# Eight quarter transfers for the input weights, another order of the hand-written schedule for pairs 0 to 17, and value transfers without unread bytes

## The chip, the cores and the metric

The kernel runs on one core of a Trainium2 chip. The time is device time in microseconds (us), the median of three runs: 406.16 us (405.56 to 406.44). The profile is one execution seen by the hardware profiler.

## The reference

The attention is a cosine attention over 8 batches, 12 heads, 448 positions and 64 channels; it is followed by a feed-forward layer with a hard-swish.

```python
q_n = q / (np.linalg.norm(q, axis=-1, keepdims=True) + 1e-06)
k_n = k / (np.linalg.norm(k, axis=-1, keepdims=True) + 1e-06)
scores = np.matmul(q_n, k_n.transpose(0, 1, 3, 2)) / tau          # tau = 0.1
attn = np.exp(scores - max) ; attn = attn / (sum + 1e-09)
x = heads side by side of np.matmul(attn, v)                       # 3584 x 768
h = x @ w_in                                                       # 768 x 2048
return (h * np.clip(h + 3.0, 0.0, 6.0) / 6.0) @ w_out              # 2048 x 768
```

## The kernel before

**Units of work.** Two heads are handled together: a "pair". There are 6 pairs to a batch and 48 in all. The queries and keys come in as items: item j holds the queries or the keys of two neighbouring pairs (2 x 7 x 64 float32 values on each of 128 partitions), so pairs 0 and 1 need items 0 and 1, pairs 2 and 3 items 2 and 3, and so on.

**The steps of an item.** `load_qk` (LQ) fetches it, `square` (SQ) squares it on the engine that its letter names (a = ScalarE, p = GpSimd, v = VectorE) and over the chunks that its numbers name, `reduce` (RE) sums the squares on VectorE, `norms` (NO) turns the sums of two items into inverse norms with four small ScalarE activations, `normalise` (NM) multiplies, and `transposes` (TR) turns the item over on TensorE into a bank of PSUM. `copy_q`, `copy_k` and `copy_k3` (CQ, CK, CS) bring the result to SBUF. Items from 14 on are turned by a DMA instead (XD).

**The steps of a pair.** `scores` (SC, groups 0 to 3) multiplies keys by queries, `exps` (EX) takes the exponential on ScalarE, `values` (VA) multiplies by the values, which `load_v` (LV) fetched and `vcast` (VC) turned into bf16, `finish_values` (FI) divides by the sums on VectorE, and `back` with `copy_x` (BK, CX), or a DMA (XP, XB), puts the result into `xT`, the input of the feed-forward layer.

**The feed-forward layer.** A unit (U) of the stream is a `mm1_unit`, six matmuls for 128 of the 2048 hidden columns of one batch; UA is its ScalarE part and UV its VectorE part. The first can start only when all six pairs of batch 0 are in `xT`. Units 31 to 36 are `mm2_unit`s, which read `w_out`. W (`next_weights`) issues the next weight transfer, cast to bf16 on the way, from GpSimd's queue. A check while the program is built, in `mm1_unit`, says how many transfers must have been issued before a unit.

**Order.** Every engine runs its own instructions in the order in which they are issued. The order of pairs 0 to 17 is written out in the list `PLAN`, one word for each step with its numbers behind dots; from pair 18 on a loop issues the rest. DP and D (`busy_pv`, `busy`) are matmuls of zeros that nobody reads, 248 and 512 columns wide. OPEN ends the start: until then two score buffers (SC0 and SC1, two PSUM banks each) take the scores in turn, so that a score must wait for the exponential before the last; from then on the four banks and the banks Y and Z form a ring of six. The word SC.i.g.n names the score buffer n, TR.j.Y the bank Y.

**Memory.** All raw items, their squares and the raw values lie in one SBUF tile, `big`: seven places for items, two for squares (items of even and odd number), three for values. So SQ of item j must wait for RE of item j - 2, LQ of item j for NM of item j - 7, and LV of d (for pairs 2d and 2d + 1) for the casts of the values three before.

Of the kernel before, what the change touches and what calls it, by code (L numbers as in the profile page):

```python
# [8 lines left out]
FP32 = mybir.dt.float32  # L9
BF16 = mybir.dt.bfloat16  # L10
AF = mybir.ActivationFunctionType
# [50 lines left out]
def kernel(  # L62
# [76 lines left out]
    def raw_buffer(j):  # L139
# [4 lines left out]
    n2s = [const.tile([128, 2, 14], FP32, name=f"n2{i}", tag=f"n2{i}") for i in range(2)]  # L144
    rs = [
        [const.tile([128, 2, 14], FP32, name=f"{x}{i}", tag=f"{x}{i}") for x in ("ln", "nr", "le", "r")]
        for i in range(2)
# [19 lines left out]
    def needs(*what):  # L167
        for w in what:
            assert w in issued or any(x < 0 for x in w[1:] if isinstance(x, int)), w
# [31 lines left out]
    def load_v(d):  # L201
        needs(("VC", 2 * (d - NV)), ("VC", 2 * (d - NV) + 1))
        b, n = 2 * d // HP, 2 * d % HP
        for g in range(2):
            f = v[b, HP * g + n : HP * g + n + 2].rearrange("i (p c) d -> p i (c d)", c=7)
            t = vr[d % NV][:, 2 * g : 2 * g + 2, :, :].rearrange("p i c d -> p i (c d)")
            for half in range(2):
                o = t[64 * half : 64 * half + 64, :, (1 - half) * D : (5 - half) * D]
                nc.sync.dma_start(out=o, in_=f[:, :, 3 * half * D : (3 * half + 4) * D])
# [18 lines left out]
    def reduce(j, *heads):  # L228
# [6 lines left out]
        else:  # L235
# [3 lines left out]
            out=n2s[d % 2][:, j % 2, c],  # L239
# [6 lines left out]
    def norms(d, *items):  # L246
# [7 lines left out]
        ln, nr, le, r = (t[:, it, :] for t in rs[d % 2])  # L254
        nc.scalar.activation(out=ln, in_=n2s[d % 2][:, it, :], func=AF.Ln)
# [7 lines left out]
        for x in items:  # L263
            issued.add(("NO", d, x))

    def normalise(j, e, *heads):
# [10 lines left out]
            in1=rs[d % 2][3][:, j % 2, :]  # L277
# [36 lines left out]
    def transposes(j, bank=None):  # L314
        nrm = nrm_of.pop(j)
# [245 lines left out]
    def mm1_unit(b, fc):  # L561
        needs(*(("CX", i) for i in range(b * HP, (b + 1) * HP)))
        assert len(weights) <= 6 - 2 * (2 * fc // FCN)
# [534 lines left out]
```

## Time and profile before

| what | value |
|---|---|
| median of three runs | 406.16 us (405.56 to 406.44) |
| span of the profiled execution, first to last instruction | 403.1 us |
| median less that span | 3.06 us |
| TensorE matmul busy (PE) | 395.5 us, 98% |
| VectorE (DVE) / ScalarE (ACT) / GpSimd (POOL) busy | 286.4 / 278.3 / 234.0 us |
| mean granted TensorE clock | 1.000 |
| first transposes / first unit on PE | 10.17 / 42.85 us |

The profile gives no device time of its own for the profiled execution beyond its span; the 3.06 us are what lies around it in the timed runs, as far as can be told. Busy PE time counts the zero matmuls too (86 of DP, 10 of D). SP issues the plain DMAs and the DMA transposes; GpSimd issues the weights.

### The profile page before, as it was taken

The page shows a single profiled execution, that of the slowest core. Times are in us where ns is not written, and L with a number is a line of the kernel's source. Part 1 is how long each engine was busy: PE and PEld are TensorE (multiplying, and loading weights), DVE is VectorE, ACT ScalarE, POOL GpSimd, SP SyncE. Part 2 cuts the span into 40 slices and gives each one's busy share as a digit, 9 for nine tenths or more (in the row PEclk, how much of TensorE's full clock was granted, in tenths as well). Part 3 has the DMA queues.
Part 4 walks back from the last instruction along what each step waited for, and adds up shares of the span by engine and source line. Part 5 has one row for each costly group of instructions (what it writes and reads, how often), then busy time and mean ns, then how long its engine had stood idle before and what let it go on. Part 6 is the DMA issues. An engine that isn't in the chain of part 4 may idle for free.

```text
span 403.1 us, 9619 instructions
## 1 busy us (share of the span) xinstructions
PE 395.5 (98%) x3696; PEld 234.3 (58%) x3696; DVE 286.4 (71%) x503; ACT 278.3 (69%) x609; POOL 234.0 (58%) x228
## 2 busy tenths in 40 slices
PE   7999999999999999999999999999999999999996
PEld 4666656555655556556555556555565556555563
DVE  5898768766998777776867888687656566644663
ACT  5999998798467686786858768668658755225230
POOL 7799655662384997488386865766665500510070
PEclk9999999999999999999999999999999999999999
DMA  8999989979988659786989659976963523130134
GB/s 289 281 254 257 216 247 230 156 125 230 187 213 220 139 128 228 171 222 130 180 216 212 152 130 164 182 192 145 192 154 76 112 46 67 41 79 21 26 73 99
DMA packets 91566, 65.32 MB, mean 162 GB/s; under 512 B 56064, under 2 KB 89984, under 8 KB 91520
## 3 DMA queue, kind: packets, MB, share of 16 engines
q1 hardware_dynamic: 87408, 58.02, 62.8%
q0 software_dynamic: 3712, 6.29, 9.0%
q8 instruction: 29, 0.48, 0.5%
q10 hardware_dynamic: 400, 0.39, 0.3%
q14 instruction: 17, 0.14, 0.1%
HBM read 47.19 MB, written 11.01 MB: 144 GB/s over the span
## 4 chain that ended last, share of the span: by engine, by line
PE 94%; DVE 3%; DMA 1%; ACT 0%; issue 0%; DVEq 0%; ACTq 0%
PE M L567 24%; PE M L740 17%; PE PV L462 13%; PE Y L567 6%; PE M L422 6%; PE Z L567 5%; PE Y L740 4%; PE Z L740 4%; PE M L614 3%; PE M L820 2%; PE Z L422 2%; PE PV L922 2%; PE Z L820 1%; PE Y L422 1%; DVE n L238 1%; PE SC L422 1%
## 5 line engine op out<-in xcount | busy, mean ns | idle before, releaser
L440 ACT ACTIVATE at<-M 128x448 bf16<-128x448 f32 x200 | 99.9, 568 | 16.4 <-PE M L422 14.4
L567 PE MATMUL M<-xT,w_in_sb 128*128 128x448 bf16 x522 | 110.8, 352 | 0.0
L567 PEld LDWEIGHTS <-w_in_sb 128*128 128x128 bf16 x768 | 72.0, 98 | 62.6 <-issue 2.8
L274 POOL TENSOR_TENSOR nrm<-big,r 128x896 bf16<-128x896 f32 (+1 forms) x48 | 79.5, 1662 | 26.1 <-ACT r L262 19.3
L576 ACT ACTIVATE u<-M,bias 128x448 bf16<-128x448 f32 x87 | 57.0, 655 | 25.2 <-PE M L567 24.8
L582 DVE SCALAR_TENSOR_TENSOR gT<-u,M 128x448 bf16<-128x448 bf16 x76 | 46.7, 618 | 36.8 <-ACT u L576 36.3
L226 POOL TENSOR_TENSOR big<-big 128x896 f32<-128x896 f32 (+3 forms) x39 | 63.9, 1641 | 10.9 <-DMA big<-in_k_dram 5.7
L462 PEld LDWEIGHTS <-at 128*128 128x128 bf16 (+1 forms) x1536 | 54.9, 97 | 22.8 <-issue 13.5
L462 PE MATMUL PV<-vx,at 128*128 128x65 bf16 (+1 forms) x1536 | 64.3, 194 | 0.2 <-DVE on L483 0.2
L238 DVE TENSOR_REDUCE n<-big 128x14 f32<-128x896 f32 (+1 forms) x50 | 51.7, 1041 | 5.6 <-ACT big L224 4.6
L379 POOL COPY km<-tT 64x128 bf16<-64x128 bf16 x34 | 12.8, 376 | 58.1 <-DMA tT<-nrm 45.1
L769 POOL TENSOR_TENSOR big<-big 128x384 f32<-128x384 f32 x11 | 11.8, 1076 | 54.6 <-ACT big L788 54.5
L740 PEld LDWEIGHTS <-gT 128*128 128x128 bf16 x288 | 27.8, 98 | 20.0 <-DVE gT L718 0.6
L740 PE MATMUL M<-w_out_sb,gT 128*128 128x384 bf16 x208 | 37.9, 326 | 0.1
L440 ACT ACTIVATE at<-Z 128x448 bf16<-128x448 f32 x49 | 27.7, 565 | 9.9 <-PE M L422 7.3
L483 DVE TENSOR_TENSOR on<-PV,rc 128x512 bf16<-128x512 f32 x48 | 33.2, 691 | 1.7
L293 POOL CAST vx<-big 128x512 bf16<-128x512 f32 x44 | 33.2, 757 | 1.2 <-DMA big<-in_v_dram 1.1
L422 PE MATMUL M<-tT,kz 64*128 64x448 bf16 (+1 forms) x175 | 31.6, 351 | 0.0
L740 PEld LDWEIGHTS <-gs 128*128 128x128 bf16 x224 | 21.5, 98 | 14.8 <-DVE gs L718 0.4
L567 PE MATMUL Y<-xT,w_in_sb 128*128 128x448 bf16 x132 | 28.6, 352 | 0.0
L440 ACT ACTIVATE at<-Y 128x448 bf16<-128x448 f32 x45 | 25.7, 570 | 3.1 <-PE Z L422 1.7
L740 PE MATMUL M<-w_sum,gs 128*128 128x384 bf16 x144 | 26.3, 326 | 0.0
(130 smaller groups left out, 561.7 us busy)
## 6 DMA issues: line engine op xcount, KB each, us to landing
big<-in_v_dram SPq DMA_DIRECT2D x96, 128.0 KB, 4.4
big<-in_k_dram SPq DMA_DIRECT2D x24, 448.0 KB, 4.9
big<-in_q_dram SPq DMA_DIRECT2D x24, 448.0 KB, 4.4
out_dram<-o SPq DMA_DIRECT2D x107, 96.0 KB, 2.2
w_in_sb<-in_moe_w_in_dram POOLq DMA_DIRECT2D x4, 768.0 KB, 10.2
w_out_sb<-in_moe_w_out_dram POOLq DMA_DIRECT2D x4, 768.0 KB, 9.2
tT<-nrm SPq DMA_TRANSPOSE x34, 3.3
xT<-on SPq DMA_TRANSPOSE x25, 3.8
```

Of the source, the lines that this page charges most:

```text
L226: engines[e].tensor_tensor(out=o, in0=i, in1=i, op=ALU.mult)
L238: nc.vector.tensor_reduce(out=n2s[d % 2][:, j % 2, c], in_=sq[:, :, :, :].rearrange("p g c d -> p (g c) d")[:, c, :], axis=AX.X, op=ALU.add,)
L274: engines[e].tensor_tensor(out=nrm[:, :, g, :].rearrange("p c g d -> p g c d"), in0=raw_of[j][:, g, :, :], in1=rs[d % 2][3][:, j % 2, :] . ...
L293: (engines[e].copy if e == "a" else engines[e].tensor_copy)(out=o, in_=f)
L422: nc.tensor.matmul(o, ks, qt[rows], start=True, stop=True)
L440: nc.scalar.activation(out=o, in_=x, func=AF.Exp, scale=inv_tau)
L462: nc.tensor.matmul(pv_out(j, h), at[rows, n, q_cols(i // HP, j)], vt[rows, 3 + h if name == "M" else 5 * h + int(name[1]), :], start=(name ...
L483: nc.vector.tensor_tensor(out=on[:, :, :, :].rearrange("p j h d -> p h j d"), in0=pv4[:, :, :, 0:D], in1=rc[:, :, :].to_broadcast([128, 2, ...
L567: nc.tensor.matmul(ps[:, 0:S], w_in_sb[:, cc, fc * 128 : (fc + 1) * 128], x[:, cc, 0:S], start=(cc == 0), stop=(cc == CC - 1),)
L576: nc.scalar.activation(out=u[:, :], in_=ps[:, 0:S], func=AF.Relu, bias=half_bias, scale=1.0 / 6.0)
L582: nc.vector.scalar_tensor_tensor(out=g[:, fc, c0 : c0 + S], in0=u[:, :], scalar=1.0, in1=ps[:, 0:S], op0=ALU.min, op1=ALU.mult,)
L740: nc.tensor.matmul(m, lhs[:, c, :], rhs[:, c, c0 : c0 + width], start=(base is None and c == 0), stop=(c == KC - 1), skip_group_check=True,)
```

## The change

- **Order.** `PLAN` is replaced. It has the same steps for pairs 0 to 17, with these differences: DP stands for 91 matmuls instead of 86 and D for 1 instead of 10; some squares are cut in two and given to two engines; SQ of items 6 and half of 7 and the second half of NM of items 1 and 5 are on VectorE; four norms (items 4 to 11) do their last two operations on VectorE (`NO.d.v`); the norms of items 12 to 15 and of 16 to 19 are taken four items at a time (the new `norms_two`, NN, on ScalarE and VectorE); seven CK and three CX are on ScalarE.
- **Weights.** `w_in` comes in eight transfers of a quarter of its columns (for each 64-row half) instead of four of a half, so W occurs twelve times. The check in `mm1_unit` follows.
- **Values.** `load_v` leaves out the 64 channels x 2 heads that `vcast` never reads: of the four transfers of each LV two bring 3 chunks instead of 4.
- **Norm tiles.** The small tiles of the norms for even and odd d lie in one tile each, padded from 14 to 16 columns.

```diff
@@ -19,42 +19,44 @@
 PLAN = [
-    "LQ.1 DP.5 SQ.1.a.11.3 SQ.1.p.4.3 DP.1 SQ.1.a.0.4 LQ.0 SQ.0.p.8.6 DP.2 DP.4 LQ.3 LQ.2 SQ.1.v.7.4 RE.1.1",
-    "SQ.0.a.0.6 RE.1.0 NO.0.1 LQ.5 LQ.4 SQ.0.v.6.2 DP.6 NM.1.p.0 D.10 RE.0.1 DP.3 NM.1.p.1 RE.0.0 DP.8 NO.0.0",
-    "SQ.3.a.0.7 LV.0 DP.2 SQ.2.a.0.7 NM.0.p.0 RE.3 RE.2 NM.0.p.1 TR.1.Y DP.2 TR.0.Z CK.0.v DP.4 SQ.4.p.0.7 CQ.0.v",
-    "SQ.5.a.0.7 LQ.6 NO.1 LV.1 LQ.7 SC.0.0.0 SC.0.1.1 DP.5 DP.3 CQ.1.v EX.0.0 RE.5 RE.4 NM.3.p SC.0.2.0 CK.1.v DP.3",
-    "EX.0.1 DP.3 EX.0.2 NM.2.v DP.3 SC.0.3.1 TR.3.Y LQ.8 NO.2 EX.0.3 DP.3 SC.1.0.0 TR.2.Z EX.1.0 VC.0.v SC.1.1.1 DP.2",
-    "EX.1.1 VA.0.0 CK.2.v VC.1.v VC.3.v NM.4.p NM.5.p VA.0.1 LQ.9 SC.1.2.0 SQ.6.a.0.7 LQ.11 DP.5 DP.2 SC.1.3.1 EX.1.2",
-    "CQ.2.v LQ.10 LV.2 VA.0.2 VA.0.3 DP.3 SC.2.0.0 DP.2 EX.1.3 CK.3.v SC.2.1.1 EX.2.0 TR.4.Y SC.2.2.0 SQ.7.p.0.7",
-    "EX.2.1 RE.6 FI.0 RE.7 LV.3 VA.1.0 SQ.8.p.0.7 SC.2.3.1 CQ.3.v VC.2.v CQ.5.v VA.1.1 EX.2.2 SC.3.0.0 EX.2.3 VA.1.2",
-    "NO.3 RE.8 SC.3.1.1 CQ.4.v EX.3.0 DP.2 DP.4 EX.3.1 VA.1.3 TR.5.Z SC.3.2.0 W SQ.9.p.0.7 EX.3.2 FI.1 CK.4.v BK.0.Y",
-    "VA.2.0 SC.3.3.1 RE.9 LV.4 EX.3.3 NO.4 VA.2.1 VA.2.2 VA.2.3 SC.4.0.0 EX.4.0 NM.6.p DP.2 SC.4.1.1 SQ.10.p.0.7 W",
-    "SQ.11.p.0.7 EX.4.1 CX.0.v TR.6.Y CK.5.v FI.2 CQ.7.v VA.3.0 BK.2.Z RE.10 SC.4.2.0 EX.4.2 NM.7.p CQ.6.v VA.3.1",
-    "SC.4.3.1 DP.2 EX.4.3 CX.2.v SC.5.0.0 RE.11 VA.3.2 EX.5.0 SC.5.1.1 VA.3.3 VC.4.p SC.5.2.0 FI.3 VC.5.p EX.5.1",
-    "BK.1.Y TR.7.Z SC.5.3.1 CX.1.v CK.6.v CK.7.v VA.4.0 EX.5.2 DP.2 CS.7.v EX.5.3 BK.3.Y VA.4.1 LQ.12 CS.6.v OPEN",
-    "DP.2 CX.3.v NO.5 SC.6.0 VA.4.2 VA.4.3 SC.6.1 SC.6.2 EX.6.0 NM.8.p FI.4 EX.6.1 EX.6.2 SC.6.3 TR.8 BK.4 VA.5.0",
-    "CX.4.v VA.5.1 CQ.8.v SC.7.0 VA.5.2 EX.6.3 NM.9.p CQ.9.v VC.6.p VA.5.3 SC.7.1 FI.5 EX.7.0 SC.7.2 TR.9 SC.7.3",
-    "NM.10.p CK.8.v VA.6.0 EX.7.1 EX.7.2 VC.8.p CS.8.v W BK.5 SQ.12.p.0.7 LQ.13 VA.6.1 VA.6.2 SC.8.0 EX.7.3 CS.9.v",
-    "VA.6.3 CK.9.v DP.1 EX.8.0 CX.5.v SC.8.1 SC.8.2 VC.7.p FI.6 LQ.15 EX.8.1 U UA SQ.13.a.0.7 LV.5 U TR.10 EX.8.2 UA",
...
+    "DP.2 DP.1 DP.1 DP.1 DP.3 DP.1 LQ.1 SQ.1.a.4.3 DP.2 DP.2 DP.2 DP.1 DP.1 SQ.1.p.11.3 DP.1 SQ.1.v.0.4 SQ.1.a.7.4",
+    "DP.2 LQ.0 DP.1 SQ.0.a.0.6 D.1 DP.3 LQ.3 DP.1 DP.1 DP.3 DP.2 DP.3 RE.1.0 DP.3 SQ.0.p.6.2 SQ.0.p.8.6 DP.1 RE.1.1",
+    "SQ.3.p.4.3 RE.0.0 LQ.2 DP.1 RE.0.1 NO.0.1 NM.1.p.0 NM.1.v.1 DP.1 DP.1 LQ.5 SQ.3.a.0.4 TR.1.Y NO.0.0 DP.1 DP.2",
+    "NM.0.p.1 DP.1 LQ.4 RE.3 DP.1 DP.1 DP.2 NM.0.p.0 SQ.2.a.0.7 RE.2 DP.1 DP.3 DP.1 TR.0.Z SQ.5.a.0.4 DP.2 DP.1",
+    "SQ.5.a.4.3 RE.5 CQ.0.v DP.1 DP.3 NO.1 DP.1 CK.0.a SQ.4.p.4.3 SC.0.0.0 SQ.4.a.0.4 EX.0.0 DP.4 LV.0 LQ.6 LQ.8",
+    "CK.1.v VC.0.v CQ.1.v SC.0.1.1 VC.1.v SC.0.2.0 EX.0.1 NM.3.p NM.2.p RE.4 SQ.6.v.0.7 DP.1 DP.1 DP.1 LQ.7 DP.1 DP.2",
+    "EX.0.2 SC.0.3.1 EX.0.3 SQ.7.p.4.3 NO.2.v NM.4.p TR.3.Y RE.6 SC.1.0.0 EX.1.0 SC.1.1.1 LV.1 VA.0.0 TR.2.Z SC.1.2.0",
+    "EX.1.1 CK.2.v CQ.2.v VA.0.1 NM.5.p.0 DP.1 EX.1.2 DP.1 W CQ.3.v LQ.9 VA.0.2 VA.0.3 FI.0 LQ.10 SQ.8.a.0.7 SC.1.3.1",
+    "CK.3.v EX.1.3 SC.2.0.0 VC.3.p DP.1 EX.2.0 SQ.7.v.0.4 RE.7 NM.5.v.1 DP.1 VA.1.0 W RE.8 SC.2.1.1 EX.2.1 DP.1",
+    "VA.1.1 DP.1 SC.2.2.0 SQ.9.p.0.7 DP.1 DP.2 SC.2.3.1 EX.2.2 EX.2.3 VA.1.2 DP.2 VC.2.v SC.3.0.0 NO.3.v SC.3.1.1",
+    "VA.1.3 DP.2 DP.1 SQ.10.p.0.7 DP.1 NM.6.p LV.2 VC.5.p FI.1 EX.3.0 EX.3.1 TR.5.Z RE.9 TR.4.Y CK.4.a SC.3.2.0 LQ.11",
+    "CQ.4.v EX.3.2 LQ.13 SQ.11.p.0.7 NM.7.p CQ.5.v SC.3.3.1 CK.5.v DP.1 NO.4.v VA.2.0 DP.1 VA.2.1 VA.2.2 LV.3",
+    "SC.4.0.0 VA.2.3 FI.2 EX.3.3 SC.4.1.1 TR.6.Y EX.4.0 BK.0.Z SC.4.2.0 RE.10 CQ.6.v DP.1 CX.0.v VC.4.p VA.3.0 EX.4.1",
+    "SC.4.3.1 VA.3.1 EX.4.2 EX.4.3 NM.8.p SC.5.0.0 SC.5.1.1 EX.5.0 VA.3.2 CQ.7.v VA.3.3 VC.7.p RE.11 FI.3 W BK.2.Y",
+    "TR.7.Z W SC.5.2.0 EX.5.1 SC.5.3.1 CK.6.v VA.4.0 CX.2.a CK.7.v BK.1.Y CS.7.v DP.1 CS.6.v EX.5.2 EX.5.3 LQ.12",
+    "BK.3.Z VA.4.1 CX.3.v NM.9.p OPEN LV.4 SC.6.0 VA.4.2 CX.1.v LQ.15 VA.4.3 FI.4 NO.5.v W SC.6.1 EX.6.0 LV.5 NM.10.p",
+    "SQ.13.p.0.7 SC.6.2 SC.6.3 TR.8 CQ.8.v EX.6.1 BK.4 CX.4.v EX.6.2 EX.6.3 VA.5.0 VA.5.1 LQ.16 VA.5.2 SQ.12.p.0.7",
+    "VC.6.v CQ.9.v SC.7.0 EX.7.0 VA.5.3 VC.9.p SC.7.1 SC.7.2 FI.5 LQ.14 TR.9 SC.7.3 CK.9.v NM.11.p CS.8.v CK.8.v",
+    "EX.7.1 VC.8.p VA.6.0 BK.5 VA.6.1 CS.9.v VA.6.2 CX.5.v VA.6.3 FI.6 EX.7.2 SC.8.0 U EX.7.3 TR.10 CQ.10.v EX.8.0",
+    "LV.6 VC.10.p UA UV SC.8.1 EX.8.1 CQ.11.v SC.8.2 EX.8.2 VA.7.0 VA.7.1 VA.7.2 W SC.8.3 VA.7.3 SC.9.0 U SC.9.1 FI.7",
+    "RE.12 LQ.18 EX.8.3 EX.9.0 XP.6 UA UV SC.9.2 U VA.8.0 EX.9.1 UA VA.8.1 TR.11 CK.10.a RE.13 EX.9.2 U UA CS.10.v",
+    "SC.9.3 CK.11.v UV UV SQ.15.p.0.7 CS.11.v EX.9.3 VA.8.2 VA.8.3 SQ.14.p.4.3 FI.8 U U UA UV UA VA.9.0 SC.10.0",
+    "SQ.14.a.0.4 VC.11.p LV.8 W W VC.12.p EX.10.0 U VA.9.1 UV RE.14 SQ.16.p.6.1 SC.10.1 UA SQ.16.p.0.6 UV EX.10.1",
+    "SC.10.2 RE.15 NN.6.v EX.10.2 NM.12.p RE.16 VA.9.2 LQ.17 VA.9.3 NM.13.p U UA U NM.14.p U SC.10.3 EX.10.3 UV U U",
...
 ]
@@ -141,10 +143,8 @@
 
     sqs = [item(NR + i) for i in range(2)]
     nrms = [const.tile([128, 7, 2, D], BF16, name=f"nrm{i}", tag=f"nrm{i}") for i in range(3)]
-    n2s = [const.tile([128, 2, 14], FP32, name=f"n2{i}", tag=f"n2{i}") for i in range(2)]
-    rs = [
-        [const.tile([128, 2, 14], FP32, name=f"{x}{i}", tag=f"{x}{i}") for x in ("ln", "nr", "le", "r")]
-        for i in range(2)
+    n2_and_r = [
+        const.tile([128, 2, 2, 16], FP32, name=x, tag=x)[:, :, :, 0:14] for x in ("n2", "ln", "nr", "le", "r")
     ]
     bias = const.tile([128, 2], FP32, name="bias", tag="bias")
     eps_bias, half_bias = bias[:, 0:1], bias[:, 1:2]
@@ -205,8 +205,11 @@
             f = v[b, HP * g + n : HP * g + n + 2].rearrange("i (p c) d -> p i (c d)", c=7)
             t = vr[d % NV][:, 2 * g : 2 * g + 2, :, :].rearrange("p i c d -> p i (c d)")
             for half in range(2):
-                o = t[64 * half : 64 * half + 64, :, (1 - half) * D : (5 - half) * D]
-                nc.sync.dma_start(out=o, in_=f[:, :, 3 * half * D : (3 * half + 4) * D])
+                n_c = 4 if g == half else 3
+                c0 = (7 - n_c) * half
+                x = 1 if g != half or half == 0 else 0
+                o = t[64 * half : 64 * half + 64, :, x * D : (x + n_c) * D]
+                nc.sync.dma_start(out=o, in_=f[:, :, c0 * D : (c0 + n_c) * D])
 
     def square(j, e, c0, n):
 
@@ -236,7 +239,7 @@
             assert sorted(have) == list(range(7))
         c = slice(7 * heads[0], 7 * heads[-1] + 7)
         nc.vector.tensor_reduce(
-            out=n2s[d % 2][:, j % 2, c],
+            out=n2_and_r[0][:, d % 2, j % 2, c],
             in_=sq[:, :, :, :].rearrange("p g c d -> p (g c) d")[:, c, :],
             axis=AX.X,
             op=ALU.add,
@@ -251,8 +254,19 @@
         for x in items:
             needs(("RE", 2 * d + x))
         it = slice(items[0], items[-1] + 1)
-        ln, nr, le, r = (t[:, it, :] for t in rs[d % 2])
-        nc.scalar.activation(out=ln, in_=n2s[d % 2][:, it, :], func=AF.Ln)
+        inverse([t[:, d % 2, it, :] for t in n2_and_r], on_vector)
+        for x in items:
+            issued.add(("NO", d, x))
+
+    def norms_two(d, on_vector=None):
+
+        needs(*(("NM", 2 * d + x) for x in range(-4, 0)), *(("RE", 2 * d + x) for x in range(4)))
+        inverse([t.rearrange("p e i c -> p (e i) c") for t in n2_and_r], on_vector)
+        issued.update(("NO", x, y) for x in (d, d + 1) for y in range(2))
+
+    def inverse(tiles, on_vector):
+        n2, ln, nr, le, r = tiles
+        nc.scalar.activation(out=ln, in_=n2, func=AF.Ln)
         nc.scalar.activation(out=nr, in_=ln, func=AF.Exp, scale=0.5)
         if on_vector:
             nc.vector.tensor_scalar(out=le, in0=nr, scalar1=EPS, scalar2=None, op0=ALU.add)
@@ -260,8 +274,6 @@
         else:
             nc.scalar.activation(out=le, in_=nr, func=AF.Ln, bias=eps_bias)
             nc.scalar.activation(out=r, in_=le, func=AF.Exp, scale=-1.0)
-        for x in items:
-            issued.add(("NO", d, x))
 
     def normalise(j, e, *heads):
         d = j // 2
@@ -274,7 +286,7 @@
         engines[e].tensor_tensor(
             out=nrm[:, :, g, :].rearrange("p c g d -> p g c d"),
             in0=raw_of[j][:, g, :, :],
-            in1=rs[d % 2][3][:, j % 2, :]
+            in1=n2_and_r[4][:, d % 2, j % 2, :]
             .rearrange("p (g c) -> p g c", g=2)[:, g, :]
             .to_broadcast([128, n, 7, D]),
             op=ALU.mult,
@@ -312,6 +324,7 @@
         return 4 if j % 2 else 2
 
     def transposes(j, bank=None):
+        needs(("NM", j))
         nrm = nrm_of.pop(j)
         z, key = bank_of(bank, readers(j))
         z = z[:, :].bitcast(BF16)
@@ -560,7 +573,7 @@
 
     def mm1_unit(b, fc):
         needs(*(("CX", i) for i in range(b * HP, (b + 1) * HP)))
-        assert len(weights) <= 6 - 2 * (2 * fc // FCN)
+        assert len(weights) <= 10 - 2 * (4 * fc // FCN)
         x, g, c0 = xT[b % 2], g_of(b), b % 2 * SR
         ps, key = bank_of(None, 1)
         for cc in range(CC):
@@ -898,10 +911,10 @@
     units[NP] += [(product_unit, n, x, 2) for n, x in ((9, "7"), (9, "6"), (10, "6"))]
     units[NP] += [(product_unit, 10, "7", x) for x in range(2)]
 
-    FG = d_ff // 2
+    FG = d_ff // 4
     weights = [
         (w_in_sb[64 * g : 64 * g + 64, :, f * FG : (f + 1) * FG], w_in_r[g, :, :, f * FG : (f + 1) * FG])
-        for f in range(2)
+        for f in range(4)
         for g in range(2)
     ] + [(w_out_sb[:, 4 * f : 4 * f + 4, :], w_out_r[:, 4 * f : 4 * f + 4, :]) for f in range(4)]
 
@@ -945,7 +958,7 @@
                     finish_units(e)
 
     OPS = {
-        "LQ": load_qk, "LV": load_v, "W": next_weights, "SQ": square, "RE": reduce, "NO": norms,
+        "LQ": load_qk, "LV": load_v, "W": next_weights, "SQ": square, "RE": reduce, "NO": norms, "NN": norms_two,
         "NM": normalise, "VC": vcast, "TR": transposes, "XD": crossbar, "XB": back_crossbar, "XP": back_two, "CQ": copy_q, "CK": copy_k, "CS": copy_k3, "SC": scores,
         "EX": exps, "VA": values, "FI": finish_values, "BK": back, "CX": copy_x, "U": unit, "UA": lambda: finish_units("a"), "UV": lambda: finish_units("v"),
         "GL": g_left, "WS": lambda x, *h: weight_sums(str(x), *((h[0] * KC // 2, KC // 2) if h else (0, KC))), "UU": whole_units, "D": busy, "DP": busy_pv, "OPEN": open_ring,
```

33 rows, old and new, of the table PLAN are left out of this document.

## The prediction

> **What bounds the kernel now.** I read the page first, for the span and for where matmuls lack.
>
> ```profile
> span 403.1 us, 9619 instructions
> PE   7999999999999999999999999999999999999996
> PEclk9999999999999999999999999999999999999999
> ```
>
> TensorE (PE) is full in all slices but the first and the last. From about 35 us to 399 us only real matmuls follow one another (DP comes once more, at 42.14 us), and the list of waits has no wait of PE or of its weight loads there above 0.6 us. The order of pairs can therefore gain only before that point, and can lose anywhere. So I asked for the stages of the start, and then for each engine's timeline in them.
>
> ```profile
> 4.30:12.87 8.57, 7.92 (x58) 5.15 (x55) 6.39 (x12) 6.64 (x19) 6.16 (x7) 1.00 1.07 343
> 12.87:35.16 22.29, 21.85 (x286) 14.25 (x285) 19.79 (x39) 21.22 (x39) 20.96 (x16) 1.00 1.06 267
> 35.16:42.85 7.69, 7.69 (x138) 5.21 (x134) 5.95 (x22) 7.53 (x21) 7.68 (x8) 1.00 1.11 247
> ```
>
> The columns are busy us of PE, weight loads, DVE, ACT and POOL. In the middle stage ACT is busy 95% of the time, and PE's share holds zero matmuls.
>
> ```profile
> 12.87 2.54 ACT L440 ACTIVATE at<-SC 128x896 bf16<-128x896 f32 x3
> 28.99 6.17 ACT L440 ACTIVATE at<-SC 128x896 bf16<-128x896 f32 x8
> 35.03 0.23 ACT L255 ACTIVATE ln<-n 128x28 f32<-128x28 f32 x1
> 10.17 0.55 PE L319 MATMUL Y<-ident,nrm 128*128 128x128 bf16 x7
> 12.47 0.55 PE L422 MATMUL SC<-tT,kz 64*128 64x448 bf16 x4 [0.65 <-DVE tT L341]
> 35.72 0.36 PE L422 MATMUL M<-tT,kz 64*128 64x448 bf16 x2
> 42.85 2.43 PE L567 MATMUL M<-xT,w_in_sb 128*128 128x448 bf16 x12
> ```
>
> ACT takes EX.0.0 at 12.87 and is done with EX.5.3 at 35.1; OPEN waits for that, and SC.6.0 starts at 35.72. From there PE has no gap to unit 1 at 42.85, and none later. The chain of the start is: item 1 lands (4.29), squares, norms, first scores, ACT through six pairs, SC.6.0, then PE alone.
>
> **The start to EX.0.0.** The second half of NM.1 moves to DVE, and PE's zeros ahead of TR.1 fall from 31 + 10 to 41 + 1. The zeros start at 2.48; 18 took 3.69 us (2.48 to 6.17, 0.205 each, cold), 13 later ones 1.38 (8.79 to 10.17, 0.106 each). The ten wide ones between took 2.62, which by their width is 2 at the slow and 8 at the fast rate, so the rate changed at about 7.1. By these, 22 of the new ones are slow and the last ends at about 9.25. NM.1 is ready at about 9.1: RE.1 at 6.0 and four norm activations to 7.07 as before, SQ.3.p (384 columns, 0.83) now ahead of NM.1.p.0 on POOL, and the other half (0.6) on DVE. So TR.1 comes 0.9 us earlier. That buys little: NM.0 still ends at 10.5 to 10.9 on POOL. What follows is RE.2 (1.05), NO.1 (1.06), CK.0 on ACT (0.5) and SQ.4.a (0.5) ahead of EX.0.0, which I place at 12.75 to 13.25 against 12.87: nothing gained, but NO.1, RE.5 and half of SQ.4 are already done. I take 13.0.
>
> **ACT from EX.0.0 to EX.5.3.** Eight exponentials (two pairs) take 35.03 - 28.99 = 6.04 us, so a pair costs 3.02 and six 18.1. Before: + NO.2, 3, 4 at 1.06 (27.93 to 28.99) = 3.2, + SQ.6 0.87 = 22.2, as seen. After: 18.1 + three norms of two activations, 0.52 each = 1.6, + SQ.8.a 0.87, + CK.4.a and CX.2.a at 0.45 = 21.5. If ACT has no wait, EX.5.3 ends at 13.0 + 21.5 = 34.5 and SC.6.0 starts at 34.6; the two zeros that stood before it (34.73, 35.41) are one now. I followed the suppliers by their rows (RE 1.03, CQ or CK on DVE 0.31, FI 0.9, NM on POOL 1.65): SC.2.0.0 is ready 0.9 before ACT wants it, SC.3.0.0 1.0, SC.4.0.0 0.5, the tightest.
>
> **PE from SC.6.0 to unit 1.** Before: 42.85 - 35.72 = 7.13, with SC.8.1, SC.8.2 (0.30 each) and a zero inside; after 6.43 without them. Unit 1 would start at 41.0; it needs CX.5, which follows TR.9 and four copies, at 41.2. Before, for equal work: 42.85 - 0.6 = 42.25. The gain is 1.05 us; later nothing can be gained, as PE is full.
>
> **The rest.** Each w_in transfer kept 384 rows, so four more cost POOL 4 x 0.70 = 2.8 us; two lie where POOL waits for RE.7 anyway, two more lie before NM.9.p, which TR.9 needs at 38.8. Units I place by adding PE's rows from SC.6.0 on (unit 1.14, score group 0.30, value group 0.30, transposes 0.40), weight issues by adding POOL's (1.65 for an NM or SQ, 0.6 for a cast, 0.70 for an issue). W3 and W4 come about 14 us before unit 5, W7 and W8 about 11 us before unit 13, against a median landing of 10.2 us: hidden, for a half of the bytes each. W12 comes about 14 us before unit 31. The value transfers shed 1/8 of 12.6 MB, 1.6 of 65.3 MB; no PE wait names them: 0. Merged norms (NN) and ACT copies lie beside full PE: 0.
>
> **A row that speaks against it.**
>
> ```profile
> 4.31 0.42 DVE L226 TENSOR_TENSOR big<-big 128x256 f32<-128x256 f32 x1 [0.81 <-DMA big<-in_k_dram]
> 5.56 0.83 POOL L226 TENSOR_TENSOR big<-big 128x384 f32<-128x384 f32 x1 [0.46 <-DMA big<-in_q_dram]
> 5.91 0.63 DVE L226 TENSOR_TENSOR big<-big 128x128 f32<-128x128 f32 x1
> ```
>
> A square of half the size took half as long again on DVE while POOL squared: it ended 0.15 after POOL's. The second row of this kind is NM.2.v, 1.26 beside POOL against 1.08 at 98.30. So DVE work with two SBUF inputs waits for POOL's, and the change puts four such pieces in the start (NM.1.v.1, SQ.6.v, SQ.7.v, NM.5.v.1), where POOL is 94% busy. The bounds are 0 each and one POOL operation each (0.83 to 1.69). I take 0.8 for one, because two of them start where POOL waits for a reduce or issues weights. The Trainium skill, "SBUF — State Buffer", section "SBUF: two separate sides", says the same as a rule: the shared port pair is an exclusive lock for the whole instruction. The trace agrees (0.63 for 0.42); taken at its worst it gives the first rival.
>
> **The rivals.**
> 1. Slower: VectorE becomes the bound of the start by those four waits. If they meet full POOL operations, they add up to about 2.9 us over what I took before CQ.4, which SC.4.0.0 and so EX.4.0 need; the slack there is 0.5 to 1.0. ACT stands still about 2.2, and the end is at 406.16 - 1.05 + 2.2 = 407.3. It turns the sign from about 1.8 us of wait in all. For it: DVE is 89% busy there already. Against: the old NM.2.v lost only 0.18.
> 2. No change: LQ.13 now stands before LV.3 in SP's queue and waits for NM.6.p (about 27.2). LV.3 is then issued to 30.5 and lands between 33.1 (2.6, the shortest landing) and 37 (6.8, the early median). VC.7.p (0.6), two weight issues (1.4) and NM.9.p (1.65) follow on POOL, so TR.9, wanted at 38.8, is late from a landing at 35.2 on. A landing at 36 takes 0.8 of the gain: 405.9. Against: SP has stood still, so the DMA queues are short.
> 3. Slower by weights: W6 is issued at about 48, and unit 9 wants it at 57. The longest w_in landing was 13.7 us: unit 9 at 61.7, 409.8. It holds only if a quarter lands no sooner than a half.
>
> **How the numbers follow.** The sum is against the profiled span: 403.1 - 1.05 = 402.05; with the 3.06 us between span and median, 405.1. Timed runs of before differ by 0.9 us, so 0.2%, or 0.81 us, is about what a measurement can tell from no change; faster means below 405.35. Chances: the forecast 0.52, rival 1 0.23, rival 2 0.17, rival 3 0.08. The forecast's own range is 404.4 (EX.0.0 at 12.75, fewer waits, PE full at once) to 405.7 (EX.0.0 at 13.25 and CX.5 late); 0.07 of its chance lies within 0.2%. Faster: 0.45 + 0.02 of rival 2 = 0.47. Same: 0.07 + 0.11 of rival 2 + 0.02 of rival 1 = 0.20. Slower: 0.21 + 0.04 + 0.08 = 0.33. The range goes from 404.4 to 407.6, which leaves out rival 3 and the ends of rival 1.
>
> **What would show it.** Right: NM.1's second half ends near 9, EX.0.0 at 12.75 to 13.25, no ACT idle time above 0.3 us up to EX.5.3 near 34.5, SC.6.0 near 34.6, unit 1 near 41.2, no PE wait after it, GpSimd's weight issues eight times near 0.70. Rival 1 shows as DVE squares and multiplies far above 1.08 and 0.6 and as ACT idle time before EX.3.3 to EX.4.0; rival 2 as a PE gap before TR.9; rival 3 as a PE wait on w_in_sb at unit 9. A gap of PE anywhere past 42 us makes the prediction wrong.

## The result, and the profile after

The changed kernel is slower: 410.35 us (median of four runs, 409.28 to 415.8) against 406.02 us for the kernel before in the same runs (405.56 to 406.44). The ratio is 1.0099, with a 95% interval of 1.0072 to 1.0125. The ratios here and below leave out executions that were disturbed: the one at 415.8 us, one of four in experiment 3, and six of ten in experiment 10, its profiled one among them. The profiled execution took 409.32 us and has a span of 407.5 us, 4.4 more than before. Forecast were 405.1 us and a range of 404.4 to 407.6.

The page of the changed kernel, its span and two rows of 40 slices:

```profile
span 407.5 us, 9625 instructions
PE   7998979999999999999999999999999999999996
PEclk9999998999999999999999999999999999999999
```

Two slices of PE below 9 (31 to 41 us and 51 to 61 us) and one of the clock (61 to 71 us) are new. The same stages as before, and the one behind them (span of the stage, then busy us of PE, weight loads, DVE, ACT and POOL, granted clock, DMA share, GB/s):

```profile
4.30:12.87 8.57, 8.57 (x74) 6.75 (x72) 8.05 (x12) 7.39 (x22) 7.63 (x9) 1.00 1.06 350
12.87:35.16 22.29, 20.79 (x297) 13.66 (x297) 20.89 (x49) 21.27 (x37) 20.20 (x19) 1.00 1.02 257
35.16:42.85 7.69, 6.49 (x106) 4.50 (x103) 7.23 (x19) 6.58 (x15) 7.33 (x6) 1.00 1.15 231
42.85:60.00 17.15, 14.91 (x172) 8.57 (x170) 13.24 (x27) 14.13 (x31) 12.01 (x15) 1.00 1.27 191
```

The rows of ACT and PE that answer to those shown of before (start, duration, instruction, idle time before it and its releaser):

```profile
12.85 2.99 ACT L453 ACTIVATE at<-SC 128x896 bf16<-128x896 f32 x4 [0.20 <-PE SC L435]
...
33.20 0.26 ACT L269 ACTIVATE ln<-n 128x28 f32<-128x28 f32 x1
...
9.35 0.56 PE L332 MATMUL Y<-ident,nrm 128*128 128x128 bf16 x7
...
33.52 0.38 PE L509 MATMUL Z<-ident,on 128*128 128x128 bf16 x4 [0.72 <-DVE kz L354]
...
34.08 0.36 PE L435 MATMUL M<-tT,kz 64*128 64x448 bf16 x2
...
39.35 0.35 PE L435 MATMUL M<-tT,kz 64*128 64x448 bf16 x1 [1.20 <-DVE tT L354]
...
41.83 1.31 PE L580 MATMUL Y<-xT,w_in_sb 128*128 128x448 bf16 x6
...
60.63 3.49 PE L580 MATMUL M<-xT,w_in_sb 128*128 128x448 bf16 x12 [2.87 <-DVE gT L595]
```

The start came at least as early as forecast: EX.0.0 at 12.85, ACT through with EX.5.3 at 33.20, SC.6.0 at 34.08, 1.64 us earlier than before. The last wait ahead of SC.6.0 is for VectorE and not for ACT: BK.3 stands 0.72 us at 33.52 for the copies out of bank Z. Then PE waits 1.20 us at 39.35, so unit 1 comes at 41.83. The large loss is past the start: PE stands still for 2.87 us before unit 9, and the twelve matmuls there take 3.49 us; before, twelve took 2.43. From SC.6.0 on the list of PE's waits (total, times, longest) has three entries; before, it had none there:

```profile
PE M L580 <- DVE gT L595: 2.9, 1, 2.9
...
PE M L435 <- DVE tT L354: 1.2, 1, 1.2
...
PE PV L475 <- DVE on L496: 0.5, 1, 0.5
```

The stretches of 2 us around unit 9 show what a standstill costs afterwards:

```profile
58.00:60.00 2.00, 0.00 (x0) 0.00 (x0) 1.57 (x4) 1.72 (x5) 0.80 (x1) 1.00 1.18 195
60.00:62.00 2.00, 1.37 (x7) 0.71 (x8) 1.39 (x4) 0.00 (x0) 2.00 (x2) 0.96 1.19 229
62.00:64.00 2.00, 2.00 (x7) 0.84 (x6) 0.00 (x0) 0.00 (x0) 2.00 (x2) 0.50 1.18 248
64.00:66.00 2.00, 2.00 (x9) 0.91 (x8) 0.37 (x1) 1.47 (x3) 1.98 (x4) 0.69 1.14 231
```

The granted clock falls to a half from about 61.8 to 65.2 us (0.04 x 2 / 0.5 = 0.16 us of the second row and 0.31 x 2 / 0.5 = 1.24 of the last), 3.4 us in all, which costs 1.7 us of full-speed work. The Trainium skill, "TensorE: Matmul & The Clock Gate", Part 1, gives 3.4 us as the window over which the clock is decided and lets it fall after an idle window; the length of the slow stretch agrees, but a standstill of 2.87 us was enough here.

The trace puts the wait at unit 9 down to gT, and a product into gT does end just ahead of it, at 60.58:

```profile
59.98 0.60 DVE L595 SCALAR_TENSOR_TENSOR gT<-u,M 128x448 bf16<-128x448 bf16 x1
```

But a weight transfer lands as near. The sixth w_in transfer is issued on POOL at 46.60 and takes 13.9 us, so it lands at 60.5 (experiment 1 separates the two):

```profile
46.60 0.69 POOL L923 DMA_DIRECT2D w_in_sb<-in_moe_w_in_dram  x1
```

The DMA issues of 46 to 48 us (KB, us from issue to landing), and then the whole kernel's:

```profile
w_in_sb<-in_moe_w_in_dram POOLq DMA_DIRECT2D x1, 384.0 KB, 13.9
xT<-on SPq DMA_TRANSPOSE x1, 13.8
...
w_in_sb<-in_moe_w_in_dram POOLq DMA_DIRECT2D x8, 384.0 KB, 11.0
```

So the sum over the profiled span is: unit 1 comes 0.42 us earlier for equal work (42.25, from the prediction, less 41.83); the standstill costs 2.87, the half clock 1.7, the wait for the division at 105.77 0.52: 4.67 us, against 4.4 seen at the end.

### The profile page after: what moved, and what is told of

Read it like the earlier page. It is cut to its first block, busy times and chain, and to the rows that moved or that the text cites. A ratio compares the mean times of both kernels' runs of the same rounds, so it can differ in the third digit from the quotient of the medians.

```text
span 407.5 us, 9625 instructions
## 1 busy us (share of the span) xinstructions
PE 394.9 (97%) x3692; PEld 235.0 (58%) x3692; DVE 292.2 (72%) x515; ACT 275.6 (68%) x594; POOL 233.3 (57%) x234
## 4 chain that ended last, share of the span: by engine, by line
PE 84%; DVE 6%; DMA 3%; POOL 2%; ACT 1%; SPq 1%; issue 1%; DVEq 0%; ACTq 0%; POOLq 0%
PE M L580 22%; PE M L753 17%; PE PV L475 11%; PE Y L580 6%; PE Z L580 6%; PE M L435 5%; PE Y L753 4%; PE Z L753 4%; POOL nrm L286 2%; PE M L833 2%; DVE n L241 1%; DMA big<-in_k_dram 1%; PE M L627 1%; PE Z L833 1%; PE Y L435 1%; DMA tT<-nrm 1%
## 5 line engine op out<-in xcount | busy, mean ns | idle before, releaser
L453 ACT ACTIVATE at<-M 128x448 bf16<-128x448 f32 x204 | 101.6, 565 | 20.4 <-PE M L435 18.0
L580 PE MATMUL M<-xT,w_in_sb 128*128 128x448 bf16 x498 | 106.2, 355 | 2.9 <-DVE gT L595 2.9
L286 POOL TENSOR_TENSOR nrm<-big,r 128x896 bf16<-128x896 f32 (+1 forms) x47 | 78.0, 1666 | 20.5 <-DVE r L273 10.5
L229 POOL TENSOR_TENSOR big<-big 128x896 f32<-128x896 f32 (+5 forms) x45 | 66.2, 1475 | 19.5 <-DVE n L241 12.9
L595 DVE SCALAR_TENSOR_TENSOR gT<-u,M 128x448 bf16<-128x448 bf16 x72 | 44.3, 619 | 39.2 <-ACT u L589 38.7
L589 ACT ACTIVATE u<-M,bias 128x448 bf16<-128x448 f32 x83 | 54.2, 654 | 25.6 <-PE M L580 25.2
L580 PE MATMUL Y<-xT,w_in_sb 128*128 128x448 bf16 x144 | 31.2, 353 | 0.0
L453 ACT ACTIVATE at<-Z 128x448 bf16<-128x448 f32 x45 | 25.4, 564 | 7.1 <-PE M L435 7.1
L305 POOL CAST vx<-big 128x512 bf16<-128x512 f32 x41 | 28.9, 706 | 2.1 <-DMA big<-in_v_dram 2.0
L580 PE MATMUL Z<-xT,w_in_sb 128*128 128x448 bf16 x126 | 27.8, 357 | 0.0
```

The source lines that it names most:

```text
L229: engines[e].tensor_tensor(out=o, in0=i, in1=i, op=ALU.mult)
L286: engines[e].tensor_tensor(out=nrm[:, :, g, :].rearrange("p c g d -> p g c d"), in0=raw_of[j][:, g, :, :], in1=n2_and_r[4][:, d % 2, j % 2, :]
L305: (engines[e].copy if e == "a" else engines[e].tensor_copy)(out=o, in_=f)
L453: nc.scalar.activation(out=o, in_=x, func=AF.Exp, scale=inv_tau)
L580: nc.tensor.matmul(ps[:, 0:S], w_in_sb[:, cc, fc * 128 : (fc + 1) * 128], x[:, cc, 0:S], start=(cc == 0), stop=(cc == CC - 1),)
L589: nc.scalar.activation(out=u[:, :], in_=ps[:, 0:S], func=AF.Relu, bias=half_bias, scale=1.0 / 6.0)
```

## The experiments

Theory A says that the loss is the late sixth weight transfer and the half clock behind it; theory B, that the wait is for VectorE, as the trace names it. Each kernel was timed against the kernel before beside it. Lines of the schedule are wrapped anew by some edits; the diffs show the words that change.

**1. The sixth weight transfer early** (the changed kernel, the transfer issued directly behind the fifth).

```diff
-    "... VA.4.3 FI.4 NO.5.v W SC.6.1 EX.6.0 LV.5 NM.10.p",
+    "... VA.4.3 FI.4 NO.5.v W W SC.6.1 EX.6.0 LV.5 NM.10.p",
...
-    "... VA.7.0 VA.7.1 VA.7.2 W SC.8.3 VA.7.3 ...",
+    "... VA.7.0 VA.7.1 VA.7.2 SC.8.3 VA.7.3 ...",
```

> The kernel after, with one word moved: the sixth W directly behind the fifth (issue near 38 instead of 46.6 us). Theory A (unit 9 waits for the sixth weight transfer, which lands 13.9 us after its issue at 46.6): the 2.9 us gap of PE before unit 9 is gone, the half clock behind it (61 to 65 us) too, and the span falls from 407.5 to 402.5-403.0, the time to 404.5-405.0. Theory B (the wait is for the VectorE product that the trace names as the releaser, behind two reduces and the norms of four items): the gap stays above 2 us and the time stays at 409-410.

Measured: 405.49 us, ratio 0.9994 (0.9969 to 1.0019), span 403.4. POOL's and PE's rows:

```profile
37.51 1.35 POOL L923 DMA_DIRECT2D w_in_sb<-in_moe_w_in_dram  x2
...
39.53 0.35 PE L435 MATMUL M<-tT,kz 64*128 64x448 bf16 x1 [0.47 <-DVE tT L354]
...
56.65 3.57 PE L580 MATMUL M<-xT,w_in_sb 128*128 128x448 bf16 x18
```

Eighteen matmuls run through unit 9 without a gap, and the clock is full. The product into gT still starts at 60.17, when unit 9 has been running since about 57.8 (56.65 and one unit of 1.14), so theory B falls: the releaser that the trace named was wrong. The time is 0.5 us above what was expected: taking the loss away gives the time of before, not the gain. Unit 1 comes only 0.24 us earlier than before (42.01 against 42.25), and the wait at 101.36 (0.64) takes more than that. SC.6.0 is at 34.99 here and was at 34.08 in the changed kernel, although the program is the same up to there, so 0.9 us of the start differ from one execution to the next.

**2. Half transfers in the new order.**

```diff
-    FG = d_ff // 4
+    FG = d_ff // 2
...
-        for f in range(4)
+        for f in range(2)
...
-        assert len(weights) <= 10 - 2 * (4 * fc // FCN)
+        assert len(weights) <= 6 - 2 * (2 * fc // FCN)
```

The fifth to the eighth W are taken out of the schedule.

> The kernel after, with the input weights in four half transfers again, at the places of the first four W; the fifth to eighth W are dropped. Theory A: every half is issued by 36 us and lands before unit 9, so as in e1 the gap and the half clock go: span 402.5-403.0, time 404.5-405.0; what it adds over e1 is 2.8 us less GpSimd work, worth 0 to -0.3. Theory B (VectorE order): no change, 409-410.

Measured: 407.52 us, ratio 1.0043 (1.0018 to 1.0068): a miss. Unit 9 has no wait, but another one opens. POOL and PE:

```profile
37.31 0.61 POOL L305 CAST vx<-big 128x512 bf16<-128x512 f32 x1 [3.34 <-DMA big<-in_v_dram]
37.86 1.35 POOL L923 DMA_DIRECT2D w_in_sb<-in_moe_w_in_dram  x2
39.22 3.35 POOL L286 TENSOR_TENSOR nrm<-big,r 128x896 bf16<-128x896 f32 x2
...
40.98 0.93 PE L332 MATMUL Z<-ident,nrm 128*128 128x128 bf16 x7 [1.75 <-POOL nrm L286]
```

This is the second rival of the prediction, with its chain: LV.3 lands late, VC.7.p waits 3.34 us, two weight issues and NM.9.p follow, and TR.9 is late. The granted clock is 0.50 from 41 to 44 us (0.87 on the mean from 35.16 to 42.85), so a gap of 1.75 us brought the half clock too. With quarters the same cast waited 0.69 us. In these two executions the new order of the start needs the smaller first transfers.

**3. The gap filled** (50 matmuls of the identity, 128 columns wide, that nobody reads, ahead of the ninth unit of the changed kernel).

```diff
+    def busy_ident(n):
+        for _ in range(n):
+            nc.tensor.matmul(PV[:, 0, 260:388], ident[:, :], ident[:, :], start=False, stop=False, ...)
...
-    "... VA.9.3 NM.13.p U UA U NM.14.p U SC.10.3 ...",
+    "... VA.9.3 NM.13.p U UA DI.50 U NM.14.p U SC.10.3 ...",
```

> The kernel after, with 50 matmuls of the identity by itself (128 columns, 0.056 us each, into columns of PV that nobody reads) on PE just before unit 9. It adds 2.8 us of useless PE work where PE stands still now and takes no wait away. If the gap itself is all that is lost: no change, 409-410. If PE also loses its clock because it stood still: unit 9 starts at 60.6 as before but at the full clock, and 1.6 to 2.0 us come back: span near 405.7, time near 407.5-408.

Measured: 411.64 us, ratio 1.0109 (1.0045 to 1.0173): a miss in time. PE's row at unit 9, then one stretch of 2 us:

```profile
61.13 2.43 PE L580 MATMUL M<-xT,w_in_sb 128*128 128x448 bf16 x12 [0.74 <-DMA w_in_sb<-in_moe_w_in_dram]
```

```profile
62.00:64.00 2.00, 2.00 (x13) 1.01 (x11) 0.00 (x0) 0.21 (x1) 2.00 (x3) 1.00 1.18 243
```

The clock stays full, the twelve matmuls take 2.43 again, and the trace now names the transfer itself. From unit 9 to the transposes of BK.8 PE takes 4.73 us instead of 6.41, 1.7 us less, which is the price of the half clock. But the 1.7 us don't arrive at the end: this execution has new PE waits at 79.50 (0.59) and from 90.38 to 91.44 (0.26, 0.18 and 0.19, all put down to gT), and its first second-layer product of the loop starts at 125.31 against 124.65. VectorE is later there because transfers land later: for a DMA transpose (item 14, 78.48 instead of 73.64) VectorE stands 1.21 us, and for values ACT stands 3.07 us, so that the next products into gT come late. First VectorE's row, then ACT's:

```profile
78.57 0.35 DVE L382 COPY kz<-tT 128x384 bf16<-128x384 bf16 x1 [1.21 <-DMA tT<-nrm]
...
88.52 0.62 ACT L305 CAST vx<-big 128x512 bf16<-128x512 f32 x1 [3.07 <-DMA big<-in_v_dram]
```

Why the transfers are later in this execution isn't shown.

**4. The fifth norms wholly on ScalarE** (experiment 1 with `NO.5` for `NO.5.v`).

```diff
-    "... VA.4.3 FI.4 NO.5.v W W SC.6.1 EX.6.0 LV.5",
+    "... VA.4.3 FI.4 NO.5 W W SC.6.1 EX.6.0 LV.5",
```

> e1, and the norms of items 10 and 11 wholly on ScalarE again (NO.5 instead of NO.5.v). Theory: the small VectorE operation of NO.5.v waits for a whole GpSimd multiply (1.50 us at 35.94, 0.17 to 0.27 elsewhere) and so delays the copies that SC.7.1 or SC.7.2 need, 1.2 us of PE at 38.2 to 39.35. Without it the wait goes, ScalarE pays 0.54 more: -0.6 to -1.2 us against e1. Rival: the copies are held by the values' cast (VC.6.v) or by ScalarE anyway, no change against e1 (within 0.3).

Measured: 404.81 us, ratio 0.9968 (0.9947 to 0.9988). The wait at 39.35 is gone, and unit 1 comes at 41.48 although SC.6.0 is at 35.10. What the wait was made of stands in the changed kernel's rows of VectorE and of POOL:

```profile
23.70 0.17 DVE L272 TENSOR_SCALAR le<-nr 128x28 f32<-128x28 f32 x1
...
35.94 1.50 DVE L272 TENSOR_SCALAR le<-nr 128x28 f32<-128x28 f32 x1
...
35.69 1.71 POOL L286 TENSOR_TENSOR nrm<-big,r 128x896 bf16<-128x896 f32 x1
```

Adding EPS to 28 values takes 0.17 us elsewhere; at 35.94 it starts while POOL's NM.9 runs (35.69 to 37.40) and ends with it, at 37.44. CQ.8 and the copies behind it on VectorE wait, and PE waits for them. PE's wait follows the length of this operation: 1.20 us for 1.50, in experiment 9 0.93 for 1.23, and in experiment 1 0.47 for 0.78.

**5. The product of item 18 on GpSimd too** (experiment 4 with `NM.18.p` for `NM.18.v`).

```diff
-    "... SC.15.0 EX.15.0 UV SC.15.1 CK.16.v NM.18.v EX.15.1 WS.6 SC.15.2 LV.9",
+    "... SC.15.0 EX.15.0 UV SC.15.1 CK.16.v NM.18.p EX.15.1 WS.6 SC.15.2 LV.9",
```

> e4, and the multiply of item 18 on GpSimd instead of VectorE (NM.18.p for NM.18.v). Theory: the VectorE multiply (two SBUF inputs) waits for GpSimd's multiply of item 17 (2.41 us at 95.38 in e4, 1.08 alone) and holds the division that PE waits for, 0.57 us at 100.76. Without it that wait goes and the time falls by 0.3 to 0.6 us against e4, to 404.2-404.5 or 0.995-0.996 of before. Rival: the weight sum behind it (2.16 us) holds the same division, or the DMA transpose of item 18 now comes later because GpSimd does it after item 17: no change or slower than e4.

Measured: 403.89 us, ratio 0.9953 (0.9923 to 0.9983). This version is faster than the kernel before. Its ratio and that of experiment 4 lie within each other's intervals, so what this edit adds is read from the trace, where the wait for the division is gone. Its page has PE full from the second slice on again:

```profile
span 400.5 us, 9625 instructions
...
PE   7999999999999999999999999999999999999996
```

The rows of the changed kernel that the edit answers to, on VectorE and PE:

```profile
100.39 2.40 DVE L286 TENSOR_TENSOR nrm<-big,r 128x896 bf16<-128x896 f32 x1
102.71 2.16 DVE L702 TENSOR_TENSOR w_sum<-w_out_sb 128x3072 bf16<-128x3072 bf16 x1
...
105.77 0.65 PE L475 MATMUL PV<-vx,at 128*128 128x65 bf16 x16 [0.52 <-DVE on L496]
```

NM.18 took 2.40 us beside POOL's NM.17 and 1.08 before; with a weight sum behind it, FI.14's division came late for PE.

**6 and 7. The kernel before with quarters, and with the shorter value transfers.**

```diff
-    FG = d_ff // 2
+    FG = d_ff // 4
...
-        for f in range(2)
+        for f in range(4)
```

Each of the first four W of before is doubled in experiment 6, and the check follows; experiment 7 has only the new inner loop of `load_v`.

> The kernel before with the quarter transfers alone: each of its first four W becomes two. Theory A (a quarter costs GpSimd as much as a half): four more issues, 2.8 us of GpSimd's time, two of them ahead of NM.7 and two ahead of NM.9, whose transposes had 0.4 to 0.8 us to spare: PE waits for TR.7 or TR.9 and the time rises by 0.5 to 1.5 us, 1.001-1.004. All quarters are issued by 45 us, so no PE wait at unit 9. Theory B: the smaller transfers relieve the value and item loads by as much: no change (within 0.2%).

> The kernel before with the shorter value transfers alone. Theory: no PE wait names a value load, 1.6 of 65.3 MB less change nothing: 0.998-1.002. Rival: the loads of the start are bound by bytes (the DMA share is above 1 from 10 to 80 us), items and values land sooner and the start gains up to 0.5 us.

Measured: 406.21 us, ratio 1.0004 (0.9985 to 1.0023), and 405.37 us, ratio 0.9984 (0.9968 to 1.0001). Quarters alone cost nothing that can be measured; PE's longest new wait is 0.41 us, for a normalised item at 34.23. Shorter value transfers alone are worth nothing to 0.3%. So neither part alone makes the kernel before slow, and experiments 1 and 9 take the loss away by moving one word: it lies in the order. The norm tiles were not tried alone; experiments 1 and 9 have them and lose nothing. The quarters' landings are instructive too: 7.3, 8.6 and 14.0 us (shortest, median, longest) against 9.8, 10.2 and 13.7 for halves. The 14.0 is the fourth quarter's, issued at 30.17, long before the first DMA transpose.

**8. The new order with the full value transfers** (experiment 4 with the old inner loop of `load_v`).

> e4 with the full value transfers of the kernel before. Theory: in the new order the values of pairs 6 and 7 are issued late, behind item 13, and GpSimd stands still for them (0.69 us in the kernel after, 3.34 in e2, where the weights came in halves); 4 full transfers land some 0.3 to 0.5 us later, which the slack ahead of TR.9 takes: 0 to +0.5 us against e4. Rival: the whole gain of the new order hangs on the shorter transfers: back to the time of before or above it (1.000-1.003).

Measured: 407.49 us, ratio 1.003 (1.0001 to 1.0059), beyond the expected half microsecond. The twelve times spread from 404.4 to 410.3 us; the profiled execution, at 406.39, lies below their median, so its trace shows a part of the loss at most. VectorE, then PE:

```profile
96.97 0.35 DVE L379 COPY kz<-tT 128x384 bf16<-128x384 bf16 x1 [3.92 <-DMA tT<-nrm]
97.23 2.41 DVE L283 TENSOR_TENSOR nrm<-big,r 128x896 bf16<-128x896 f32 x1
99.56 2.16 DVE L699 TENSOR_TENSOR w_sum<-w_out_sb 128x3072 bf16<-128x3072 bf16 x1
...
102.62 0.65 PE L472 MATMUL PV<-vx,at 128*128 128x65 bf16 x16 [2.27 <-DVE on L493]
```

VectorE stands 3.92 us for the DMA transpose of item 16 (2.21 in experiment 4), then does NM.18.v and the weight sum, and PE waits 2.27 us for the division behind them. The granted clock stays at 1.00 behind this wait. That the transpose comes late because of the extra value bytes is likely but not shown by this one pair.

**9 to 11. What makes the sixth transfer late.** The trace of the changed kernel has a second transfer beside it: XP.6, the first DMA transpose, issued on SP at 46.33 and landed after 13.8 us. Before, it was issued at 51.28, behind the weights, and landed after 3.2 us:

```profile
xT<-on SPq DMA_TRANSPOSE x1, 3.2
```

Experiment 9 moves XP.6 back, experiment 10 moves the load of item 18, which is issued at 45.58, and experiment 11 is experiment 9 with `NO.5` and `NM.18.p`.

```diff
-    "RE.12 LQ.18 EX.8.3 EX.9.0 XP.6 UA UV SC.9.2 U VA.8.0 EX.9.1 UA VA.8.1 TR.11 CK.10.a RE.13 EX.9.2 U UA CS.10.v",
+    "RE.12 LQ.18 EX.8.3 EX.9.0 UA UV SC.9.2 U VA.8.0 EX.9.1 UA VA.8.1 TR.11 CK.10.a RE.13 EX.9.2 U UA CS.10.v",
...
-    "SC.10.2 RE.15 NN.6.v EX.10.2 NM.12.p RE.16 ...",
+    "SC.10.2 RE.15 XP.6 NN.6.v EX.10.2 NM.12.p RE.16 ...",
```

In experiment 10 LQ.18 moves from behind RE.12 to behind SQ.14.a.0.4.

> The changed kernel with its first DMA transpose (XP.6) issued some 14 us later, the sixth weight transfer left in its place. In the changed kernel the transpose is issued at 46.33 and takes 13.8 us to land, the sixth w_in transfer is issued at 46.60 and takes 13.9, and between 48 and 54 us the weight queue moves 30, 8 and 55 packets in 2 us, against 208 and 212 before, where the first transpose comes at 51.28, lands in 3.2 us and stands behind the weights. Theory A (the transpose holds up the weight transfer): the sixth transfer lands in at most 10 us, the wait of TensorE at unit 9 and the half clock behind it are gone, and the time is 405 to 406.5, ratio to before 0.998 to 1.001. Theory B (a quarter lands no sooner than a half whatever runs beside it, or the item and value loads hold it up): it lands in 13 to 14 us again, unit 9 waits over 2 us, and the time is 409 to 411.

> The changed kernel with the load of item 18, which is issued at 45.58 just ahead of the transpose and the sixth w_in transfer, moved some 13 us later; the transpose stays at about 46. Theory A (the transpose holds up the weight transfer): nothing much changes, the sixth transfer lands in 12 to 14 us, unit 9 waits 1.5 to 3 us, time 409 to 411. Theory B (the load beside it holds it up): it lands in at most 10 us, no wait at unit 9, time 405 to 406.5.

> The changed kernel with three edits: the first DMA transpose some 14 us later, the fifth norms wholly on ScalarE, and the product of item 18 on GpSimd. Theory A: as the kernel with the sixth weight transfer early and the same two other edits, 403.4 to 404.6, ratio to before 0.993 to 0.997, with no TensorE wait above 0.6 us after 34 us. Theory B: the wait of 2 to 3 us at unit 9 stays, 407 to 409.

Measured: experiment 9, 405.73 us, ratio 0.9993 (0.9976 to 1.001), span 402.1. The sixth transfer, still alone on POOL and now at 47.63, lands in 8.0 us, no w_in transfer takes more than 9.3, and PE runs through unit 9:

```profile
w_in_sb<-in_moe_w_in_dram POOLq DMA_DIRECT2D x1, 384.0 KB, 8.0
```

Experiment 10: a median of 413.97 us (407.03 to 418.3), ratio 1.0051 (1.002 to 1.0082), which fits neither theory; in its profiled execution the transpose (issued at 48.95) lands after 15.0 us and the sixth transfer (issued at 49.67) after 14.3. Experiment 11: 404.11 us, ratio 0.9966 (0.9939 to 0.9992), as theory A has it; but PE has two waits above the expected 0.6 us, 0.91 at unit 9 and 0.73 at 101.09.

So moving the transpose alone takes the loss away: its early place is what makes the sixth transfer too late. That the plain load has no part in it rests on the one profiled execution of experiment 10. By how much the transpose delays the landing is less certain. In experiment 9 the fourth transfer lands after 8.6 us, against 11.3 in the changed kernel, before either kernel issues the transpose, so a part of the difference between 8.0 and 13.9 us is that execution's own. In experiment 11 the fourth and the fifth take nearly as long as in the changed kernel (10.6 and 12.4 us against 11.3 and 13.1), and the sixth, issued at 46.15, takes 10.7. The DMA view of 52 to 54 us shows how, first of the changed kernel (busy tenths of the 16 engines in 40 slices, then packets, MB and share by queue; q0 carries the weights, q1 SP's transfers):

```profile
DMA  9330413322314133132241331392221213121313
...
q1 hardware_dynamic: 58, 0.06, 23.4%
q0 software_dynamic: 55, 0.06, 18.4%
```

And of experiment 9:

```profile
DMA  5999999996949699999997949997999999799958
...
q0 software_dynamic: 272, 0.26, 124.4%
```

In the changed kernel both transfers are outstanding and the engines are mostly idle: this isn't a want of bandwidth. Without the transpose the weights move five times as many packets. What the two transfers wait for inside the queues no view shows. Nor is the transpose all of it, as the 10.7 us and the wait of 0.91 us in experiment 11 show.

## Why the prediction was wrong, point by point

- **The start: right in its mechanism up to EX.5.3.** TR.1 9.35 (forecast 9.25), EX.0.0 12.85 (13.0), SC.6.0 34.08 (34.6). ACT's sum was 20.35 us instead of 21.5: the three norms of two activations cost 1.24 together (the first 0.40, 15.71 to 16.11), not 1.6, and a pair 2.90 ((20.35 - 1.24 - 0.84 - 0.45 - 0.41) / 6, with the square and the two copies taken off) instead of 3.02. My price made up the 22.2 of before only because a wait of 0.46 us at 21.05 stood in it. The step from EX.5.3 to SC.6.0, 0.1 us in the forecast, was 0.9: PE waited for copies on VectorE at 33.52, which my chain does not have. In the experiments with the new order SC.6.0 comes at 33.62 to 35.10 (37.45 in experiment 10), in the three kernels with the old one at 35.72 to 36.40.
- **SC.6.0 to unit 1: a term left out.** I priced the norms that go half to VectorE by what they save on ACT, and nothing for VectorE. The one at 35.94 cost PE 1.20 us, so the gain was 0.42 instead of 1.05. My row that speaks against the change listed four pieces with two SBUF inputs; the small one with one input wasn't among them. The Trainium skill, "SBUF — State Buffer", section "SBUF: two separate sides", which I used for the four, puts the lock also on VectorE operations in a two-port mode, which no run here tells apart; the row shows that one input was enough here (1.50 us against 0.17). The four pieces cost 0.7 us together (1.11, 1.09, 0.81 and 0.61 against 0.6, 1.08, 0.62 and 0.6 alone), near the 0.8 that I took, and ACT never stood: the first rival fell.
- **"The rest ... hidden": the step that failed.** I checked W3, W4, W7, W8 and W12 against a median landing of 10.2 us and costed quarters as landing no later than halves. W6, the only one with less than 11 us of lead, appears in the third rival alone, at a chance of 0.08; it took 13.9 us, and the sum has 0 where the trace has 2.87 of wait and 1.7 of half clock. And I moved XP.6 by 5 us in SP's queue without pricing it: it is not in the sum at all. By experiment 9 that move is what makes W6 too late.
- **The third rival: the right place and, by luck, the right size.** It gave 409.8 us from a wait of 4.7; the wait was 2.87 and the half clock, which it didn't have, 1.7. Its condition, that a quarter lands no sooner than a half, held in the changed kernel (median 11.0 us, longest 13.9, against 10.2 and 13.7 before) and not in experiment 9 (5.8 to 9.3).
- **The second rival** didn't occur in the changed kernel (a wait of 0.69 us on POOL, none on PE) and did with half transfers. I took the value transfers at zero; in the new order they aren't (407.49 us in experiment 8 against 404.81).
- **PE full after unit 1, so nothing to lose there: wrong.** NM.18.v cost 0.5 us at 105.77, for the reason of the four pieces, at a place that I never followed.

## What to carry to other kernels

A transfer with a deadline is judged by its longest landing and by what else is issued beside it: list the DMAs that a new order moves next to it, also those of another queue (here a DMA transpose). A gap of TensorE can cost more than its length, since the clock can fall behind it; here 2.87 us brought another 1.7, and 2.27 us in experiment 8 nothing. When a transfer lands at the moment at which a wait put down to an engine ends, move that transfer alone to see which of the two it was.

## What the runs showed of the hardware that I had not expected

- A DMA transpose and a weight transfer issued 0.3 us apart took 13.8 and 13.9 us, with the DMA engines mostly idle between 52 and 54 us. With the transpose issued behind the weight transfers it took 8.3 us (3.2 before), and the sixth weight transfer 8.0 in one execution and 10.7 in another.
- TensorE's clock was halved for about 3.4 us after standstills of 2.87 us (the changed kernel) and of 1.75 us (experiment 2), and not after one of 2.27 us (experiment 8).
- An operation of VectorE with 28 values and one SBUF input took 1.50 us beside a GpSimd multiply of 1.71, and 0.17 elsewhere.
